# Gated linear attention and a GELU MLP in one kernel: seven products of zeros instead of five ahead of the first prefix sums

## The chip, the core and the metric

The kernel runs on one core of a Trainium2 chip. The metric is device time in microseconds (us) for one execution, lower is better. The engines that matter here are TensorE (PE in the profile; PEld is its loading of the stationary operand, which overlaps the products), VectorE (DVE), ScalarE (ACT), GpSimd (POOL), and SyncE (SP), which only issues transfers. Each engine works through its own instructions in the order of the program; between engines they wait on semaphores.

## What is computed

```python
def attention(q, k, v, alpha):              # each (4, 8, 768, 48): batch, heads, tokens, head size
    for t in range(S):
        state = alpha[:, :, t, :, None] * state + einsum('bhd,bhe->bhde', k[:, :, t], v[:, :, t])
        y[:, :, t] = einsum('bhd,bhde->bhe', q[:, :, t], state)

x = y.transpose(0, 2, 1, 3).reshape(3072, 384)
out = gelu_tanh(x @ w_in) @ w_out           # w_in 384x2048, w_out 2048x384
```

The inputs and the output are float32.

## The kernel before

The tokens are cut into six chunks of 128. A chunk of two batches is a unit `m` (twelve of them, numbered in order of work; unit 0 is chunk 0 with batches 0 and 1, unit 1 is chunk 0 with batches 2 and 3). The recurrence is turned into products inside a chunk, with a carried state between chunks. For one unit the steps are, with the names that the order below uses:

- `ln`: ACT takes the logarithm of alpha, into `la` (line 349 for the first two units, which are packed differently from the rest, line 351 otherwise).
- `cum`: TensorE multiplies `la` by a triangular matrix of ones, which gives prefix sums over the tokens in `cum` (lines 336 and 340 for the first two units, seven products of up to 384 columns and four of 4 columns for one batch).
- `b`, `binv`, `bend`: ACT takes exponentials of `cum` (lines 397 and 391).
- `qp`, `kp`: DVE scales q by `b` and k by `binv` (line 408).
- `t` and `ev`: TensorE transposes `qp` and `kp` into `qkT_ps` (line 418), and ACT or DVE copies the result to `qkT` (line 436).
- `attn` and `mask`: TensorE forms the products of k and q (line 479), DVE masks them (line 486).
- `y`, `x`, `tx`, `xe`, `kv`, `st`: the output of the chunk, its transpose for the MLP, and the new state.
- `l1`, `gelu`, `l2`: the two layers of the MLP (lines 562, 568, 581), which fill most of the rest of the time.

The number behind a name is the unit, the one after the point is the batch in the unit or a running number, so `cum0.1` is the second prefix sum of unit 0.

`Scheduler.order` decides what each engine does next. For the first part of the kernel it does not decide: it follows a list that is written out by hand, `FIRST`, whose letters name the engine (`P` TensorE, `V` DVE, `A` ACT, `G` GpSimd, `S` SyncE). `LANDED` gives the times at which that list takes the loads to have landed; it does not alter the order of the list.

An entry `P:fill.n` in `FIRST` stands for `n` products of a tile of zeros with itself (`fill`, lines 274 to 280: 128x128 by 128x512 into a bank of PSUM with the name `idle`). Nothing reads their result. They take a bank of the ring `ff`, which has four; the prefix sums of the first units and the products of the MLP take banks of the same ring. `fill.5` at the head of the list is TensorE's first work and waits only for the zeros (a memset on DVE, line 849, with the one at line 853 the last that TensorE waits for). The next TensorE work behind it is `cum0.0`, which waits for `ln0.0` on ACT, which waits for the first load of alpha.

The loads: `S:load.0` to `S:load.11` are issued by SP (line 295), in the order a, a, q, k, q, k of unit 0 and the same of unit 1, each 192 KB. `G:load.12` and on are issued by POOL: v of unit 0 behind `gate.0`, then, behind `gate.1`, the first quarter of `w_in`, v of unit 1, the other quarters of `w_in`, `w_out` and the later units. A gate is a copy of one column on POOL (line 304): `gate.0` waits for the second load of alpha, `gate.1` for `qp0.1`, since it reads that tile.

The head of the list, with the entry that the change touches:

```python
FIRST = """
    A:table.0 S:load.0 S:load.1 S:load.2 S:load.3 S:load.4 A:ln0.0 S:load.5 P:fill.5 P:cum0.0 A:ln0.1 G:gate.0 G:load.12 S:load.6 P:cum0.1 A:b0.0 S:load.7
    A:binv0.0 V:qp0.0 A:bend0.0 A:b0.1 V:kp0.0 S:load.8 P:fill.2 P:t0.0 A:bend0.1 A:binv0.1 V:ev0.0 P:t0.1 S:load.9 A:ev0.1 S:load.10 V:qp0.1 P:fill.3
    P:attn0.0 V:kp0.1 P:t0.2 G:gate.1 S:load.11 G:load.13 V:mask0.1 P:fill.1 P:t0.3 G:load.14 A:ev0.3 V:end0.0 V:ev0.2 A:ln1.0 V:mask0.0 P:fill.4
    P:attn0.1 G:load.15 P:cum1.0 V:mask0.2 A:vb0.0 G:load.16 A:ln1.1 V:vb0.1 P:y0.0 V:mask0.3 A:b1.0 P:cum1.1 ...
```

Of the kernel before, what the change touches and what calls it, by code (L numbers as in the profile page):

```python
# [171 lines left out]
class _Kernel:  # L172
# [9 lines left out]
    RINGS = (('a', 0, 0, 1), ('a', 0, 1, 2), ('q', 0, 0, 1), ('k', 0, 0, 1), ('q', 0, 1, 2), ('k', 0, 1, 2),  # L182
             ('a', 1, 0, 1), ('a', 1, 1, 2), ('q', 1, 0, 1), ('k', 1, 0, 1), ('q', 1, 1, 2), ('k', 1, 1, 2))
    FIRST = """
        A:table.0 S:load.0 S:load.1 S:load.2 S:load.3 S:load.4 A:ln0.0 S:load.5 P:fill.5 P:cum0.0 A:ln0.1 G:gate.0 G:load.12 S:load.6 P:cum0.1 A:b0.0 S:load.7
        A:binv0.0 V:qp0.0 A:bend0.0 A:b0.1 V:kp0.0 S:load.8 P:fill.2 P:t0.0 A:bend0.1 A:binv0.1 V:ev0.0 P:t0.1 S:load.9 A:ev0.1 S:load.10 V:qp0.1 P:fill.3
        P:attn0.0 V:kp0.1 P:t0.2 G:gate.1 S:load.11 G:load.13 V:mask0.1 P:fill.1 P:t0.3 G:load.14 A:ev0.3 V:end0.0 V:ev0.2 A:ln1.0 V:mask0.0 P:fill.4
        P:attn0.1 G:load.15 P:cum1.0 V:mask0.2 A:vb0.0 G:load.16 A:ln1.1 V:vb0.1 P:y0.0 V:mask0.3 A:b1.0 P:cum1.1 G:load.17 A:x0.0 V:qp1.0 A:binv1.0 P:y0.1
# [711 lines left out]
```

## Time and profile before

| | us |
|---|---|
| median of six runs | 179.56 (179.27 to 179.81) |
| the profiled execution, its own time | 179.5 |
| span of the profile, first to last instruction | 177.7 |
| PE busy / PEld busy | 171.8 / 136.0 |
| ACT busy | 131.0 |
| DVE busy | 95.0 |
| POOL busy | 57.8 |

The span is 1.8 us shorter than the execution's own time. The times in the views below are counted from the start of the span. A timeline row gives the start, the time from the start of its first instruction to the end of its last, the engine, the line, the operation, what it writes and reads, the shape and the number of instructions merged in the row; in brackets stands how long the engine had been idle before it and what ended that. The products of TensorE are pipelined, so one that follows another starts before the other's end: the time from one start to the next is shorter than the duration of one. A row of the windows gives, for a stretch of the span, the busy time of PE, PEld, DVE, ACT and POOL with the number of instructions, the granted clock of TensorE, the busy share of the DMA engines and GB/s.

### The profile page before, as it was taken

What the parts mean: (1) busy time and instruction counts of PE and PEld (TensorE: products, weight loads), DVE (VectorE), ACT (ScalarE), POOL (GpSimd) and SP (SyncE); (2) the same over time, 40 slices, a digit from 0 to 9 for tenths busy, and PEclk for the clock granted to TensorE, in tenths of its full rate; (3) what the DMA queues carried; (4) which work ended last, traced back from release to release, by engine and by line L of the source; (5) the groups of instructions that cost most, each with busy time, mean ns of one, the idle gap of its engine ahead of it and who ended that gap; (6) DMA issues with size and microseconds to landing.
All of it is one profiled execution on the core that took longest, in us unless ns stands there. A gap on an engine that the chain in (4) does not pass through costs nothing.

```text
span 177.7 us, 4411 instructions
## 1 busy us (share of the span) xinstructions
PE 171.8 (97%) x1831; PEld 136.0 (77%) x1831; DVE 95.0 (53%) x187; ACT 131.0 (74%) x216; POOL 57.8 (33%) x64
## 2 busy tenths in 40 slices
PE   5999999999999999999999999999999999999992
PEld 1656899666896897798698689688697697786972
DVE  6299820354967894596499797495426405000000
ACT  4567899875898668858788967977988984481831
POOL 2379336987635775767640000000000000000000
PEclk9999999999999999999999999999999999999999
DMA  4999999999999999999999993271270360401102
GB/s 118 263 271 189 194 224 233 238 245 195 237 286 203 222 266 217 196 250 212 194 252 235 196 158 93 57 175 48 46 208 4 89 162 4 130 3 48 44 3 85
DMA packets 48900, 28.86 MB, mean 162 GB/s; under 512 B 37488, under 2 KB 45296, under 8 KB 48880
## 3 DMA queue, kind: packets, MB, share of 16 engines
q0 software_dynamic: 26464, 17.70, 60.7%
q1 hardware_dynamic: 22416, 10.88, 24.9%
q8 instruction: 14, 0.23, 0.6%
q14 instruction: 6, 0.05, 0.1%
HBM read 25.17 MB, written 4.72 MB: 168 GB/s over the span
## 4 chain that ended last, share of the span: by engine, by line
PE 89%; ACT 3%; DVE 3%; DMA 2%; issue 1%; DVEq 0%
PE acc L581 35%; PE hT L562 34%; PE at L479 4%; PE qkT_ps L418 3%; PE yps L536 2%; PE yps L533 2%; PE cum L368 2%; PE kv L496 2%; DMA a<-in_alpha_dram 2%; PE cum L336 2%; DVE atm L486 1%; ACT qkT L436 1%; PE xT_ps L550 1%; PE idle L279 1%; ACT L568 1%
## 5 line engine op out<-in xcount | busy, mean ns | idle before, releaser
L581 PE MATMUL acc<-w_out,gT 128*128 128x384 bf16 (+1 forms) x400 | 69.4, 319 | 0.0
L562 PE MATMUL hT<-xT,w_in 128*128 128x256 bf16 x576 | 68.8, 273 | 0.1
L568 ACT ACTIVATE gT<-hT 128x512 bf16<-128x512 f32 x96 | 56.1, 599 | 15.1 <-PE hT L562 11.6
L562 PEld LDWEIGHTS <-w_in 128*128 128x128 bf16 x576 | 61.2, 114 | 1.5 <-issue 0.2
L581 PEld LDWEIGHTS <-gT 128*128 128x128 bf16 x400 | 36.5, 97 | 18.9
L486 DVE TENSOR_TENSOR atm<-at,ut 128x512 bf16<-128x512 f32 x48 | 30.1, 683 | 13.7 <-PE at L479 13.7
L408 DVE TENSOR_TENSOR qp<-q,b 128x768 bf16<-128x768 f32 (+1 forms) x15 | 11.9, 795 | 17.9 <-ACT b L397 17.9
L593 ACT COPY ot<-acc 128x384 f32<-128x384 f32 (+1 forms) x18 | 8.3, 461 | 13.7 <-PE acc L581 11.5
L298 POOL DMA_DIRECT2D k<-in_k_dram x11 | 12.2, 1105 | 9.1 <-DVE atm L486 3.0
L298 POOL DMA_DIRECT2D a<-in_alpha_dram x11 | 12.2, 1112 | 5.8 <-DMA w_in<-in_moe_w_in_dram 1.4
L298 POOL DMA_DIRECT2D q<-in_q_dram x11 | 12.2, 1108 | 5.3 <-issue 1.0
L298 POOL DMA_DIRECT2D vb<-in_v_dram x11 | 12.1, 1100 | 4.9 <-DMA a<-in_alpha_dram 1.2
L397 ACT ACTIVATE b<-cum 128x768 bf16<-128x768 f32 (+1 forms) x15 | 10.3, 685 | 3.3 <-PE cum L340 1.6
L270 ACT ACT_TABLE_LOAD x9 | 11.5, 1283 | 0.9 <-PEq L884 0.7
L408 DVE TENSOR_TENSOR kp<-k,binv 128x768 bf16<-128x768 f32 (+1 forms) x15 | 11.9, 791 | 0.0
L568 ACT ACT_TABLE_LOAD x9 | 11.5, 1283 | 0.2
L397 ACT ACTIVATE binv<-cum 128x768 bf16<-128x768 f32 (+1 forms) x15 | 10.2, 680 | 0.0
L518 DVE TENSOR_TENSOR stmp<-kv,st 128x384 f32<-128x384 f32 x16 | 8.8, 553 | 2.0 <-PE kv L496 2.0
L543 DVE CAST x<-yps 128x384 bf16<-128x384 f32 x12 | 6.7, 558 | 5.2 <-PE yps L536 5.2
L521 DVE TENSOR_TENSOR st<-stmp,ends 128x384 bf16<-128x384 f32 x16 | 8.9, 558 | 0.6
L436 ACT COPY qkT<-qkT_ps 128x512 bf16<-128x512 bf16 (+1 forms) x9 | 6.5, 729 | 3.4 <-PE qkT_ps L418 3.4
L351 ACT ACTIVATE la<-a 128x768 f16<-128x768 f32 (+1 forms) x11 | 8.5, 784 | 0.6 <-DMA a<-in_alpha_dram 0.5
(64 smaller groups left out, 159.0 us busy)
## 6 DMA issues: line engine op xcount, KB each, us to landing
out_dram<-ot SPq DMA_DIRECT2D x23, 192.0 KB, 2.4
a<-in_alpha_dram POOLq DMA_DIRECT2D x9, 384.0 KB, 11.8
q<-in_q_dram POOLq DMA_DIRECT2D x9, 384.0 KB, 11.7
k<-in_k_dram POOLq DMA_DIRECT2D x9, 384.0 KB, 11.7
vb<-in_v_dram POOLq DMA_DIRECT2D x9, 192.0 KB, 11.8
w_in<-in_moe_w_in_dram POOLq DMA_DIRECT2D x4, 384.0 KB, 8.7
w_out<-in_moe_w_out_dram POOLq DMA_DIRECT2D x4, 384.0 KB, 11.0
a<-in_alpha_dram SPq DMA_DIRECT2D x4, 192.0 KB, 4.1
```

The costliest lines, as they stand in the source:

```text
L270: nc.scalar.add_instruction(mybir.InstLoadActFuncSet(name=nc.get_next_instruction_name(), act_func_set_id=i, engine=mybir.EngineType.Activ ...
L298: dma(u[t][:, lo:hi].rearrange("t b h d -> t (b h) d"), src.rearrange("b h s d -> s (b h) d")[c * C:(c + 1) * C])
L351: self.nc.scalar.activation(u["la"][:, lo:hi, :, 0:self.D], u["a"][:, lo:hi], AF.Ln)
L397: self.nc.scalar.activation(u[n].rearrange("t i h d -> t i (h d)")[:, lo:hi], cum, AF.Exp, scale=1.0 if n == "b" else -1.0)
L408: self.nc.vector.tensor_tensor(out, rows, b, op=ALU.mult)
L486: self.nc.vector.tensor_tensor(u["atm", i][:, o], u["at", i][o], self.ut[:, None, :].to_broadcast([self.C, self.H // 2, self.C]), op=ALU.mult)
L518: nc.vector.tensor_tensor(s, acc, old, op=ALU.add)
L521: nc.vector.tensor_tensor(new.rearrange("f p (o d) -> f (p o) d", o=2), acc.rearrange("f p (o d) -> f (p o) d", o=2), ends, op=ALU.mult)
L562: self.nc.tensor.matmul(h[:, s], w_in[:, j, nt % 4 + s], self.xT[c % self.NX][:, j, lo:hi].rearrange("p g t -> p (g t)"), start=j == 0, st ...
L568: return lambda e: self.nc.scalar.activation(self.gT[c % self.NG][:, nt:nt + 2, lo * self.C:hi * self.C], f.pop(("h", c, lo, nt)), AF.Gelu ...
L581: self.nc.tensor.matmul(f["acc", c, b][:, lo:hi], self.gT[c % self.NG][:, nt, b * self.C:(b + 1) * self.C], self.w_out[:, nt, lo:hi], star ...
L593: self.copy(e)(f["ot", c, b][:, sl], f["acc", c, b] if half is None else f["acc", c, b, half][:, sl])
```

## The change

One number in the list is altered. The two added products come directly behind the five, ahead of `cum0.0`; TensorE gets four more instructions (two loads of the stationary operand and two products). No other engine's instructions are changed, and the order of everything else on TensorE is the same.

```diff
     FIRST = """
-        A:table.0 S:load.0 S:load.1 S:load.2 S:load.3 S:load.4 A:ln0.0 S:load.5 P:fill.5 P:cum0.0 A:ln0.1 G:gate.0 G:load.12 S:load.6 P:cum0.1 A:b0.0 S:load.7
+        A:table.0 S:load.0 S:load.1 S:load.2 S:load.3 S:load.4 A:ln0.0 S:load.5 P:fill.7 P:cum0.0 A:ln0.1 G:gate.0 G:load.12 S:load.6 P:cum0.1 A:b0.0 S:load.7
```

## The prediction

> **What bounds the kernel now.** I read the page's slices first.
>
> ```profile
> PE   5999999999999999999999999999999999999992
> PEclk9999999999999999999999999999999999999999
> ```
>
> TensorE has work in nearly every slice, so whatever delays it early is likely to reach the end. The clock row says full speed everywhere, but it can't be taken at its word for the first slices: the durations of equal work, in the timeline of TensorE alone, contradict it.
>
> ```profile
> 1.19 2.31 PE L279 MATMUL idle<-zero 128*128 128x512 bf16 x5 [1.19 <-DVE half L853]
> 4.39 1.44 PE L336 MATMUL cum<-la,ut_blk 128*128 128x384 f16 x7 [0.89 <-ACT la L349]
> 5.62 0.29 PE L340 MATMUL cum<-blk,la 128*128 128x4 f16 x4
> 5.77 1.44 PE L336 MATMUL cum<-la,ut_blk 128*128 128x384 f16 x7
> 7.00 0.29 PE L340 MATMUL cum<-blk,la 128*128 128x4 f16 x4
> 7.16 1.01 PE L279 MATMUL idle<-zero 128*128 128x512 bf16 x2
> 7.96 0.63 PE L418 MATMUL qkT_ps<-ident,qp 128*128 128x128 bf16 x4
> 8.39 0.52 PE L418 MATMUL qkT_ps<-ident,kp 128*128 128x128 bf16 x4
> 8.74 0.81 PE L279 MATMUL idle<-zero 128*128 128x512 bf16 x3
> ...
> 10.36 0.39 PE L418 MATMUL qkT_ps<-ident,kp 128*128 128x128 bf16 x4
> ...
> 11.93 0.83 PE L336 MATMUL cum<-la,ut_blk 128*128 128x384 f16 x7
> 12.60 0.24 PE L340 MATMUL cum<-blk,la 128*128 128x4 f16 x4
> 12.70 0.36 PE L536 MATMUL yps<-vb,atm 128*128 128x48 bf16 x8
> ```
>
> Seven products of one prefix sum take 1.44 us at 4.39 and 5.77 and 0.83 us at 11.93; four transposes take 0.63 at 7.96 and 0.39 at 10.36. Product by product, zeros start 0.427 us apart ahead of 3 us and 0.216 apart behind 8.74; in the row at 8.39 the last two transposes start 0.086 apart, between 0.107 before and 0.056 after. So TensorE runs at half speed until about 8.65 us, inside that row, and at full speed from there.
>
> Whether the early part counts at all, the chain that ended last and the windows tell.
>
> ```profile
> 0.74 3.06 DMA a<-in_alpha_dram
> 3.81 0.53 ACT la L349
> 4.39 1.44 PE cum L336 x7
> 5.91 1.30 PE cum L336 x7
> 7.29 0.88 PE idle L279 x2
> 8.17 0.44 PE qkT_ps L418 x4
> ```
>
> ```profile
> 23.19:120.00 96.81, 96.81 (x1099) 78.41 (x1099) 64.32 (x117) 78.05 (x125) 45.49 (x41) 1.00 1.21 208
> 120.00:174.00 54.00, 54.00 (x513) 43.52 (x511) 13.22 (x21) 37.22 (x59) 0.00 (x0) 1.00 0.25 68
> ```
>
> The chain starts with alpha's first load, then runs over both half-speed prefix sums and zeros into the transposes. From 23.19 TensorE has no idle time up to 174 us. A shift that survives to 23.19 comes through to the end.
>
> **The two products by themselves.** Five take 0.427 us from start to start ((2.31 - 0.63) / 4, 0.63 being one product's duration). The fifth starts at 2.87 and hands over at 3.30; two more end their turn at 3.30 + 2 x 0.427 = 4.15. `cum0.0` starts at 4.39, released by `ln0.0`. So 0.24 us of idle time is left, and the 0.85 us of added work is hidden under the wait for alpha (landed 3.79) and its logarithm (3.81 + 0.52). They wait for no bank (four in the ring, one taken). Direct cost: 0. Without that cover, with alpha over 0.24 us earlier, the excess would be paid, at most 0.85.
>
> **What they may move: the clock.** From 4.39 to 8.65, 4.26 us, TensorE was busy without a break, and then the clock rose. From 1.19 to 4.39 it had the five products, then a break of 1.09 (3.30 to 4.39), and the clock did not rise. With seven the break is 0.24. If a stretch of continuous work is what counts, and a break of 0.24 does not spoil it, the same 4.26 us now run from 1.19 and end at 5.45. The bounds: 5.45, or 8.65 again if the short break spoils it too. I take 5.45: the work from 5.62 to 5.77 and from 7.00 to 7.16 is four products of 4 columns each, in which the array is nearly empty for 0.15 us, and twice that did not prevent the rise at 8.65, so breaks of that size are tolerated.
>
> The Trainium skill (TensorE: Matmul & The Clock Gate, Part 1, What's actually happening) gives a rule beside this: the clock is raised after one busy window of 3413 ns, and the windows run freely, whatever the kernel does. By it the rise at 8.65 makes 5.24 the previous boundary of this execution, with the break of 1.09 in the window ahead of it; with seven that window has 0.24 idle and the rise would come at 5.24, which gives the same sum within 0.1 us. It speaks against a fixed gain, though: in another execution the boundary lies elsewhere, in both kernels, and the same section warns not to fit to a count of cold products. No run here shows that spread yet.
>
> **What an earlier clock is worth,** from 5.45. Of `cum0.0` 0.32 us are left; at full speed about 0.19: 0.13 gained. `cum0.1` with its small products takes 5.77 to 7.16, 1.39; the same work at full speed takes 11.93 to 12.70, 0.77: 0.62 gained, 0.75 in all. TensorE comes to the two zeros at 6.41 and leaves them at 6.84 (2 x 0.216). Here the next limit appears: `qp0.0` on DVE waits for `b0.0`, only 0.13 earlier, and ends at 6.47 - 0.13 + 0.56 = 6.90. So `t0.0` starts at about 6.95 instead of 7.96; `kp0.0` ends at 7.36, so `t0.1` starts at 7.40 and is done at 7.79 (0.39 each). ACT's copy starts at 7.83 instead of 8.95 and `attn0.0` at 8.47 instead of 9.59; DVE's copy starts at 7.40 instead of 8.63, and `qp0.1` at 8.01 instead of 9.24 (q landed 7.20). TensorE is some 1.1 us early at `attn0.0`.
>
> **What takes part of it back: loads.** The loads do not move with TensorE.
>
> ```profile
> 10.41 0.75 POOL L311 DMA_DIRECT2D w_in<-in_moe_w_in_dram  x1
> ...
> 11.70 0.50 ACT L379 CAST vb<-v 128x384 bf16<-128x384 f32 x1
> ...
> 12.10 0.52 ACT L349 ACTIVATE la<-a 128x384 f16<-128x384 f32 x1
> ```
>
> By the trace's landing events the last parts of v of unit 0 land at 11.10 and of the second alpha of unit 1 at 11.49. So `vb0.0` can move from 11.70 to 11.12 and `ln1.1` behind it from 12.10 to 11.52, ending at 12.04. `cum1.1` behind that starts at 12.08 instead of 12.90: 0.82 early, no longer 1.1.
>
> Those landings may slip: POOL's `gate.1` waits for `qp0.1`, so the first quarter of `w_in` is issued 1.23 earlier, 9.18 instead of 10.41, and its packets (which began some 1.2 us behind the issue) meet SP's loads. Bounds for alpha's delay: 0, if `w_in`'s packets stay behind v's, which were put on the same queue and end at 11.10; or 1.6 us, if SP's queue falls from 10.4 on to the 40% of its rate (59 against 165 KB per half us) that it had from 12.0 to 12.5, when `w_in` came up, so that the last 1.1 us take 2.7. The nearer is 0, since half of v's shares end after 10.2; I take 0.25. That leaves 0.82 - 0.25 = 0.57, about 0.6 us. Behind 13 us the chain is compute; the later weights come no later than before. The bounds of this step: 1.1 gained, or 1.0 lost (1.6 less the 0.6 of slack of `ln1.1` behind alpha).
>
> **The sum.** 179.5 - 0.6 = 178.9 us, 0.3% faster. The median of the runs is 0.06 above the profiled execution, which I leave out.
>
> **The rivals.** *Nothing moves:* the products vanish in the idle time and the clock rises where it did: 179.5. For it: the break is not fully closed, and no row shows what a 0.24 us break of no work at all does. Against: the 0.15 us stretches above. The same time comes out if the rise is early but loads eat all of it.
>
> *The loads collide (slower):* the early `gate.1` lets `w_in` run into alpha of unit 1. It decides from the point at which alpha lands later than 12.10, 0.61 behind its present 11.49; from there `ln1.1` is late, and behind it on ACT `b1.0`, `x0.0` and `binv1.0`, for which DVE's `qp1.0` and TensorE's `cum1.1` wait. With a delay of 1.1, midway between that point and the bound of 1.6, it costs 0.5: 180.0. For it: in the windows the DMA engines are 0.96 to 1.00 busy from 4.39 to 12, so there is no spare rate. Against: the queue order above.
>
> *The zeros overrun:* where alpha comes earlier than in the profiled execution, `cum0.0` waits for the seventh product. Even without any earlier clock that is a few tenths at most: 179.7.
>
> **How the numbers follow.** Forecast 0.60, nothing 0.20, collision 0.14, overrun 0.06. The forecast's own range is 178.4 (1.1 gained, no load in the way) to 179.3. The range over all cases, to hold eight in ten, reaches from 178.4 to 179.8. A measurement of this kernel can tell from no change about 0.2%, 0.36 us. Of the forecast about one tenth falls inside that and the rest is faster: 0.54 faster; nothing with that tenth and half of the overruns: 0.29 within; the rest, 0.17, slower.
>
> **What would show it.** Right: in the profile after, the first row of zeros has seven products ending near 4.35, `cum0.0` still starts near 4.39, `cum0.1` takes about 0.8 us instead of 1.44, the four transposes at about 7 us take 0.39, and `w_in` is issued near 9.2. The load step: `ln1.1` starts between 11.5 and 12. Wrong: `cum0.1` again at 1.44 (the clock did not come), `cum0.0` later than 4.45 (overrun), or the ACT row of `ln1.1` behind 12.1 with a wait for alpha (collision). A start of the long stretch of `l1` products no earlier than 23.19, in spite of an early clock, would mean that I have missed a wait between 13 and 23 us.

## The result, and the profile after

| | median, us | runs |
|---|---|---|
| before, five products | 179.44 (178.88 to 180.76) | 48 |
| after, seven products | 178.57 (177.74 to 180.00) | 24 |

The ratio is 0.995, with a 95% interval from 0.9938 to 0.9961: 0.5% faster, about 0.9 us. The profiled execution took 178.72 us, its span is 176.9 us, 0.8 us shorter than the span before.

The timeline of TensorE alone, in the profile after; the columns are start, time from first start to last end, engine, line, operation, tiles, shape, number of instructions:

```profile
1.19 3.17 PE L279 MATMUL idle<-zero 128*128 128x512 bf16 x7 [1.19 <-DVE half L853]
4.29 1.44 PE L336 MATMUL cum<-la,ut_blk 128*128 128x384 f16 x7
5.53 0.29 PE L340 MATMUL cum<-blk,la 128*128 128x4 f16 x4
5.68 1.40 PE L336 MATMUL cum<-la,ut_blk 128*128 128x384 f16 x7
6.91 0.24 PE L340 MATMUL cum<-blk,la 128*128 128x4 f16 x4
7.01 0.59 PE L279 MATMUL idle<-zero 128*128 128x512 bf16 x2
7.44 0.39 PE L418 MATMUL qkT_ps<-ident,qp 128*128 128x128 bf16 x4
7.67 0.39 PE L418 MATMUL qkT_ps<-ident,kp 128*128 128x128 bf16 x4
7.89 0.81 PE L279 MATMUL idle<-zero 128*128 128x512 bf16 x3
8.73 0.40 PE L479 MATMUL at<-qkT 64*128 64x128 bf16 x8
```

Read the durations, as before. The last of the seven products starts at 3.72 and hands over at 4.15, ahead of `cum0.0`, which starts at 4.29, some 0.1 earlier than before because alpha landed 0.09 earlier in this execution (3.70). Both prefix sums still run at half speed (1.44 and 1.40). Everything from 7.01 on runs at full speed: two products of zeros in 0.59 us instead of 1.01, four transposes in 0.39 instead of 0.63. The record of the granted clock in the trace begins at 6.90 us; before it began at 8.65. So the transposes start 0.52 earlier, the next ones 0.72, and `attn0.0` 0.86.

The loads, in the timeline of all engines after:

```profile
9.64 0.75 POOL L311 DMA_DIRECT2D w_in<-in_moe_w_in_dram  x1
...
10.89 0.50 ACT L379 CAST vb<-v 128x384 bf16<-128x384 f32 x1
...
11.29 0.52 ACT L349 ACTIVATE la<-a 128x384 f16<-128x384 f32 x1
```

The weights are issued 0.77 earlier, and neither row on ACT has a bracket, so ACT had not been idle for a load. From 11 us to the end TensorE's work stands 0.77 earlier than before, and that of DVE and ACT with it from 13 us on; TensorE again has no idle time from 23.19 to 173. So the gain is made ahead of 11 us and carried to the end.

One execution of the changed kernel, in its repeat (seven_again below), had a mean granted clock of 0.56 and took 291.74 us; no reading below rests on it.

### The profile page after: what moved, and what is told of

Same layout as the page of the kernel before. It is cut to its first block, busy times and chain, and to the rows that moved or that the text cites. A ratio compares the mean times of both kernels' runs of the same rounds, so it can differ in the third digit from the quotient of the medians.

```text
span 176.9 us, 4415 instructions
## 1 busy us (share of the span) xinstructions
PE 171.9 (97%) x1833; PEld 135.8 (77%) x1833; DVE 95.0 (54%) x187; ACT 130.9 (74%) x216; POOL 57.8 (33%) x64
## 4 chain that ended last, share of the span: by engine, by line
PE 87%; ACT 3%; DVE 3%; DMA 2%; SPq 2%; issue 1%; DVEq 0%
PE acc L581 35%; PE hT L562 35%; PE at L479 4%; PE qkT_ps L418 3%; PE yps L536 2%; DMA k<-in_k_dram 2%; PE yps L533 2%; PE cum L368 2%; PE kv L496 2%; SPq L295 2%; DVE atm L486 1%; ACT qkT L436 1%; PE xT_ps L550 1%; ACT L568 1%; PE cum L370 1%
## 5 line engine op out<-in xcount | busy, mean ns | idle before, releaser
L536 PE MATMUL yps<-vb,atm 128*128 128x48 bf16 x192 | 8.9, 183 | 0.1
L543 ACT CAST x<-yps 128x384 bf16<-128x384 f32 x12 | 5.7, 478 | 4.2 <-PE yps L536 4.2
```

The source lines that it names most:

```text
L536: nc.tensor.matmul(y[:, h, :], u["atm", i][:, h % 2, h // 2, :], u["vb"][:, i, h, :], start=c == 0, stop=True, skip_group_check=True)
L543: self.copy(e)(x, u["y", i].rearrange("t h d -> t (h d)"))
```

## The experiments

Each kernel is the changed one with the edit shown, timed beside the kernel before on the same chip; the ratios are to that kernel.

**One product instead of five.** Is it the amount of work that raises the clock, or its continuity?

```diff
-P:fill.7 P:cum0.0
+P:fill.1 P:cum0.0
```

> One product of zeros ahead of the first prefix sums instead of five, so TensorE rests from about 1.6 to 4.39 us. Theory (the clock rises after a stretch of some 3.4 us in which TensorE is hardly ever idle, and the break of 1.09 us in the kernel before spoils that stretch already): the five products did nothing, so the time stays within 0.25 us of the kernel before, about 179.4 us, and equal work behind 4.39 us has the durations of before. Rival (the clock rises after a certain amount of TensorE work, break or no break): 1.7 us of work less, the rise comes up to 1.7 us later, and the time is 0.4 to 1 us above the kernel before.

Measured: 179.34 us beside 179.41, ratio 0.9995 (0.9981 to 1.0009). Four products fewer than five make no difference, as the theory had it. TensorE alone:

```profile
1.19 0.61 PE L279 MATMUL idle<-zero 128*128 128x512 bf16 x1 [1.19 <-DVE half L853]
4.36 1.44 PE L336 MATMUL cum<-la,ut_blk 128*128 128x384 f16 x7 [2.56 <-ACT la L349]
...
8.37 0.63 PE L418 MATMUL qkT_ps<-ident,kp 128*128 128x128 bf16 x4
```

All of this is at half speed; in this execution the clock rose at 10.35. The rival, the amount of work, had asked for 0.4 to 1 us more than the kernel before, and falls. The five products of the kernel before were worth nothing that can be measured.

**Six, and nine.**

```diff
-P:fill.7 P:cum0.0
+P:fill.6 P:cum0.0      (in the other kernel P:fill.9)
```

> Six products, which leave a break of about 0.66 us ahead of the first prefix sum, where five leave 1.09 and seven 0.24. Theory (a nearly unbroken stretch is what counts): the time lies at that of five (179.4 us) or at that of seven (178.6 us) or between, as the break is or is not tolerated; between the two would mean that it depends on where the stretch falls in an execution. Rival (amount of work): half of the gain of seven, about 179.0 us, with a rise of the clock 0.43 us earlier than with five.

> Nine products: the last ends its turn at 1.19 + 9 x 0.427 = 5.03 us, so the first prefix sum starts 0.64 us later than in the kernel before, unless the clock has risen by then. Theory (unbroken stretch): the clock comes no earlier than with seven, the 0.64 us are paid in part, and the time is between that of seven and that of the kernel before, about 179.0 us. Rival (amount of work): the added work brings the clock forward again and the time is that of seven, 178.6 us, or lower.

Measured: six, 178.51 us, ratio 0.9951 (0.9934 to 0.9969); nine, 178.56 us, ratio 0.9952 (0.9937 to 0.9967). Both have the whole gain. For nine that is the time I had put down for the rival, the amount of work, not for the theory (179.0); in the profile below the rise came so early that the products cost little. Six, TensorE alone:

```profile
1.19 2.74 PE L279 MATMUL idle<-zero 128*128 128x512 bf16 x6 [1.19 <-DVE half L853]
4.31 1.44 PE L336 MATMUL cum<-la,ut_blk 128*128 128x384 f16 x7 [0.38 <-ACT la L349]
...
5.69 0.84 PE L336 MATMUL cum<-la,ut_blk 128*128 128x384 f16 x7
...
7.01 0.40 PE L418 MATMUL qkT_ps<-ident,qp 128*128 128x128 bf16 x4
7.47 0.40 PE L418 MATMUL qkT_ps<-ident,kp 128*128 128x128 bf16 x4
```

Here the second prefix sum already runs at full speed (0.84); the rise is at 5.77. A break of 0.59 us (3.72 to 4.31, from the sixth product's hand-over) is tolerated. The span of this execution is 176.5, 0.4 below that with seven. Nine, TensorE, then ACT, then DVE:

```profile
1.19 3.56 PE L279 MATMUL idle<-zero 128*128 128x512 bf16 x9 [1.19 <-DVE half L853]
4.58 0.82 PE L336 MATMUL cum<-la,ut_blk 128*128 128x384 f16 x7
...
18.96 0.37 PE L536 MATMUL yps<-vb,atm 128*128 128x48 bf16 x8 [0.53 <-DVE vb L379]
```

```profile
10.89 0.51 ACT L379 CAST vb<-v 128x384 bf16<-128x384 f32 x1 [0.38 <-DMA v<-in_v_dram]
```

```profile
18.54 0.36 DVE L379 CAST vb<-v 128x384 bf16<-128x384 f32 x1 [0.67 <-DMA v<-in_v_dram]
```

The rise is at 4.14, ahead of both prefix sums, which take 0.82 each. Nine should have been 0.64 us late; the early rise shortened the last products, and `cum0.0` starts 0.29 later than with seven. Now ACT waits 0.38 us for v of unit 0. That wait is made good: at 17 us TensorE is 1.38 ahead of the kernel before, as at `attn0.0`. What is lost is lost later: v of unit 1 lands at 18.52 (17.45 with seven), DVE waits 0.67 for it and TensorE 0.53 for DVE. From 23 us on 0.97 is left, and the span is 176.8, only 0.2 below that with seven. Loads do limit the gain, as I had predicted for seven, but at an earlier rise and through a later load.

**Four products, started later.** Less work than before, and a short break.

```diff
-nc.vector.memset(self.zero, 0.0)                          (first on DVE)
 nc.vector.tensor_reduce(self.blk, ...)
+nc.vector.memset(self.zero, 0.0)                          (behind the reduction)
-P:fill.7 P:cum0.0
+P:fill.4 P:cum0.0
```

> Four products instead of five, but they start later: the tile of zeros is cleared behind the reduction for blk on DVE instead of first, so that they run from about 2.4 to 4.1 us and the break ahead of the first prefix sum is about 0.25 us instead of 1.09. Less work than the kernel before, without the break. Theory (unbroken stretch): the clock rises earlier than before in most executions, though later than with seven, since the stretch begins 1.2 us later; the time is about half way, 178.8 to 179.1 us. Rival (amount of work): one product less than before, 179.4 us or above.

Measured: 178.87 us, ratio 0.9969 (0.9953 to 0.9985), inside the range of the theory. TensorE alone:

```profile
2.47 1.89 PE L279 MATMUL idle<-zero 128*128 128x512 bf16 x4 [2.47 <-DVE zero L856]
4.34 1.44 PE L336 MATMUL cum<-la,ut_blk 128*128 128x384 f16 x7
...
7.10 0.59 PE L279 MATMUL idle<-zero 128*128 128x512 bf16 x2
7.53 0.38 PE L418 MATMUL qkT_ps<-ident,qp 128*128 128x128 bf16 x4
```

Four products with a break of 0.2 us (the last hands over at 4.15) do more than five with one of 1.09. Together with the single product this shows that the length of the break counts and not the amount of work.

**Weights released too early.** How dear is the collision that I named as the slower rival?

```diff
-'gateqp 0 1'
+'gateqp 0 0'
```

> Seven products, and the gate in front of the weights on POOL reads the first q product of unit 0 instead of the second, so that the first quarter of w_in is issued near 7.2 us instead of 9.6. It measures the collision that I named as the slower rival. If weights that come early do delay alpha of unit 1 (the rival), alpha lands later than 11.5 and ACT waits for it: 0.3 to 1 us slower than seven. If the queue order protects it (my forecast's choice, 0.25 us of delay): within 0.3 us of seven.

Measured: twelve runs from 178.92 to 184.57 us, median 181.73, beside 179.50 for the kernel before on that chip; the five fastest of the twelve alone give a ratio of 1.0038 (1.0007 to 1.0069). The weights were issued at 7.36. The profiled execution (183.99 us), ACT, DVE and then TensorE:

```profile
11.38 0.51 ACT L379 CAST vb<-v 128x384 bf16<-128x384 f32 x1 [0.79 <-DMA v<-in_v_dram]
```

```profile
16.07 0.56 DVE L408 TENSOR_TENSOR qp<-q,b 128x384 bf16<-128x384 f32 x1 [0.89 <-DMA q<-in_q_dram]
19.09 0.56 DVE L408 TENSOR_TENSOR kp<-k,binv 128x384 bf16<-128x384 f32 x1 [2.46 <-DMA k<-in_k_dram]
```

```profile
16.01 0.40 PE L479 MATMUL at<-qkT 64*128 64x128 bf16 x8 [0.19 <-ACT qkT L436]
19.70 0.61 PE L418 MATMUL qkT_ps<-ident,kp 128*128 128x128 bf16 x4 [3.29 <-DVE kp L408]
```

Alpha is late too (it landed at 11.79, against 10.94 after), and ACT waits 0.79 us for v of unit 0. But the dear part is what stands behind alpha on SP's queue: the last k of unit 1 landed at 18.99 instead of 12.98. TensorE waits 3.29 us for it, and its next four transposes take 0.61, half speed again. The windows of that execution, cut at the clock's grid (PE busy, PEld, DVE, ACT, POOL, granted clock, DMA share, GB/s):

```profile
15.44:18.85 3.41, 0.79 (x13) 0.28 (x9) 0.56 (x1) 1.01 (x2) 1.63 (x2) 1.00 1.19 205
18.85:22.27 3.42, 2.57 (x20) 2.20 (x21) 1.84 (x4) 1.07 (x2) 1.03 (x2) 0.50 1.21 210
22.27:25.68 3.41, 3.41 (x37) 2.65 (x36) 2.11 (x4) 2.36 (x5) 1.46 (x2) 0.50 1.08 243
```

After a stretch in which TensorE was busy for 0.79 of 3.41 us the clock is at 0.50 for two stretches, 6.83 us; the first of the two was 75% busy (2.57 of 3.42) and did not bring full speed back, the second, wholly busy, did. In eight of the twelve runs the mean granted clock was 0.98 to 0.99, in the other four 1.00, and these four are the fastest (178.92 to 180.74 us). The collision is real and larger than I priced it. Weights issued at 9.64 (seven) and 8.87 (nine) do not reach it, with the last k at 12.98 and 12.80; weights issued at 7.36 do.

**The zeros in front of the transposes left out.**

```diff
-P:cum0.1 ... P:fill.2 P:t0.0
+P:cum0.1 ... P:t0.0
```

> Seven products at the head, and the two products of zeros between the second prefix sum and the first transposes are left out. Where the clock rises behind about 6.5 us those two stood in the way of the transposes (in the first profile of the changed kernel the transposes started at 7.44, and q's product had been ready at 6.93); where it rises earlier there is slack. Theory: 0.1 to 0.3 us below seven in the median. Rival (they keep the array busy, and without them the clock rises later or falls again): no gain or slower than seven, with four transposes at 0.63 us.

> The changed kernel once more, as the reference for the three others on this chip. 178.5 us, 0.4 to 0.6% below the kernel before; the clock rises at another time than the 6.90 us of its first profile, anywhere from 4.4 to 7.8 us.

Measured: 178.72 us, ratio 0.9952 (0.9936 to 0.9968), beside 178.70, ratio 0.9942 (0.992 to 0.9964), for the changed kernel on that chip, whose rise was not measured a second time. No gain: the rival's time, though not by its mechanism, since the transposes take 0.38 and 0.40. The profile says where the gain went: its rise is at 6.92, almost that of the profile after, and the transposes start at 7.02 instead of 7.44. From 13 to 18 us it is 0.42 ahead. Then TensorE meets v of unit 1 (landed 18.32, against 17.45) and the second quarter of `w_in` (20.25, against 19.20); from 23 us on it is 0.23 ahead, from 35 us 0.05, and at 102 us it falls 0.65 behind. The waits of TensorE from 24 to 176 us (who waited for whom, us in total, times, longest):

```profile
PE hT L562 <- DMA xT<-x: 0.5, 1, 0.5
```

So a gain can be given back to transfers, here to loads and to a transpose by DMA (`turn_x_dma`, line 462) that is used from unit 6 on. That is one execution; the runs show only that the median did not fall.

**Small products.** What does the clock count, time or columns?

```diff
+for _ in range(8 if n == 5 else 0):
+    self.nc.tensor.matmul(ps[:, 0:4], self.zero[:, 0:self.C], self.zero[:, 0:4], start=True, stop=True)
-P:fill.7 P:cum0.0
+P:fill.5 P:cum0.0
```

> Five products of 512 columns and behind them eight of 4 columns with the same weights, so that TensorE has instructions until about 4.1 us, but hardly a column streams through the array in the last 0.85 us. Theory A (the gate counts time in which TensorE has work of any kind, weight loads included): as with seven, 178.5 us. Theory B (it counts streaming columns): as with five, 179.4 us.

Measured: 180.69 us, ratio 1.0056 (1.0033 to 1.008): slower than five, which neither theory had. It does not answer the question. TensorE alone:

```profile
3.30 0.40 PE L281 MATMUL idle<-zero 128*128 128x4 bf16 x8
4.30 1.44 PE L338 MATMUL cum<-la,ut_blk 128*128 128x384 f16 x7 [0.61 <-DVE ut L866]
```

The eight took 0.40 us instead of 0.85, so a break of 0.6 was left (it ends where DVE's `ut` and ACT's logarithm do, both near 4.25); the rise in the profile, 7.36, can't tell the two theories apart, since the stretch of 3.41 us ahead of it begins behind the small products. And the time is not lost there: the early part is 0.2 us behind that of seven, and then TensorE waits at 102 us for the transfer that the last experiment met:

```profile
PE hT L564 <- DMA xT<-x: 1.1, 1, 1.1
```

Why that transfer is later in this kernel is open.

**Without transposes by DMA.** Does the gain depend on those transfers, and does the earlier gate cost anything? All transposes go to TensorE, once with five, once with seven products, and with seven and a later gate.

```diff
-TURN_QK, TURN_X = (7, 8, 9, 10, 11), (6, 7, 8, 9, 10, 11)
+TURN_QK, TURN_X = (), ()
-P:fill.7 P:cum0.0
+P:fill.5 P:cum0.0      (pe5 only)
-'gateqp 0 1'
+'gatekp 0 1'           (pe7_late_gate only)
```

> The kernel before with all its transposes on TensorE (TURN_QK and TURN_X empty), five products of zeros: the partner of the next kernel. The part ahead of about 60 us is the same work in the same order. TensorE gets more work later, some 5 to 8 us, so about 186 us. It is a second profile of the early part with five products: if the clock rises on a grid of about 3.4 us that runs freely, at another time than 8.65, anywhere from 7.2 to 10.7 us.

> The same with seven products. Theory (the gain is made ahead of 13 us and TensorE's later work carries it to the end, whatever that work is): 0.7 to 1.0 us faster than its partner with five, and the clock rises between 4.1 and 7.4 us. Rival (later waits for transfers take the gain or make it): a difference below 0.3 us, or above 1.5.

> Seven products, all transposes on TensorE, and the gate in front of the weights on POOL waits for the second k product of unit 0 instead of the second q product, which is 0.47 us later on DVE, so the weights meet less of SP's loads. If the earlier opening of the gate costs the seven something (the 0.25 us of the prediction's load step), this is 0.1 to 0.3 us faster than its partner with seven; if not, the same within 0.2 us or a little slower.

| | median, us | runs | ratio to the kernel before |
|---|---|---|---|
| pe5 | 185.54 (185.33 to 185.73) | 4 | 1.0336 (1.0321 to 1.035) |
| pe7 | 184.78 (184.55 to 185.44) | 5 | 1.0305 (1.0286 to 1.0324) |
| pe7_late_gate | 185.07 (184.96 to 185.31) | 4 | 1.0311 (1.0297 to 1.0326) |

By the medians seven are 0.76 us faster than five in this kernel too; with so few runs the intervals of the two just overlap. In the two profiles seven are 0.64 ahead at 24 us and 0.76 from 40 us on. So the gain does not need the transposes by DMA. Holding the weights back (10.07 instead of 9.20 in the profiles) gains nothing that can be seen, though 0.1 us would not be seen with so few runs. Five products, and then seven:

```profile
5.72 1.44 PE L336 MATMUL cum<-la,ut_blk 128*128 128x384 f16 x7
...
7.64 0.39 PE L418 MATMUL qkT_ps<-ident,qp 128*128 128x128 bf16 x4
```

```profile
5.68 0.82 PE L336 MATMUL cum<-la,ut_blk 128*128 128x384 f16 x7
...
6.99 0.40 PE L418 MATMUL qkT_ps<-ident,qp 128*128 128x128 bf16 x4
```

With five the clock rose at 7.34 this time, not at 8.65, and with seven at 5.60, not at 6.90.

**All profiles together.** The record of the clock in the trace gives each rise; the stretches at full and at half clock that follow last whole multiples of 3.4133 us (167.253, 170.666, 174.080 and 177.493 us are 49 to 52 times that; 6.827 at half clock in early_gate is twice). So I cut each profile backwards from its rise in steps of 3.41 us, and worked out how much of a stretch TensorE was busy: all of it, less the time before the zeros start (1.19, in late4 2.47) and between the last zeros' hand-over and `cum0.0`. The small products of small8 count as busy here (as idle they would make 62% of the 74%).

| kernel | rise, us | stretch ahead of the rise busy | stretch before that busy |
|---|---|---|---|
| before, five | 8.65 | 100% | 68% |
| pe5, five | 7.34 | 88% | 62% |
| fill1 | 10.35 | 100% | 75% |
| fill6 | 5.77 | 83% | 34% |
| after, seven | 6.90 | 96% | 67% |
| pe7, seven | 5.60 | 95% | 29% |
| pe7_late_gate, seven | 6.80 | 96% | 65% |
| early_gate, seven | 5.20 | 95% | 17% |
| seven_no2 | 6.92 | 96% | 68% |
| fill9 | 4.14 | 86% | none |
| late4 | 7.04 | 94% | 34% |
| small8 | 7.36 | 90% | 74% |

In these profiles the clock rises at the end of a stretch that was busy for 83% or more, and not after one of 75% or less, and where the stretches fall differs from one execution to the next. From the start of unbroken work to the rise it took from 2.95 us (fill9) to 5.99 us (fill1), so a fixed time of work does not fit. That agrees with the rule that the prediction took from the Trainium skill (TensorE: Matmul & The Clock Gate, Part 1, What's actually happening), windows of 3413 ns that run freely; the share between 75% and 83% is this case's. A table of the same section says that the clock falls after an idle window; in early_gate a window that was 23% busy was enough (0.79 of 3.41), so it need not be wholly idle.

Where no later wait takes a larger part back, the span follows the rise: 178.1 us in fill1 (10.35), 177.7 before (8.65), 177.1 in late4 (7.04), 176.9 after (6.90), 176.5 in fill6 (5.77), about 0.35 us for each us, an estimate from these five.

Further profiles of the two kernels as they stand, and the later gate on the changed kernel itself, were planned and gave no result. So each kernel has one profile, and how often the rise falls where is not measured.

## Why the prediction was right

Starts in us, the prediction beside two profiles. Six products had an execution with a rise near the one that I had assumed, so they test the working; seven are the kernel that it was made for.

| step | before | predicted | seven | six |
|---|---|---|---|---|
| rise of the clock | 8.65 | 5.45 | 6.90 | 5.77 |
| `t0.0` | 7.96 | 6.95 | 7.44 | 7.01 |
| `t0.1` | 8.39 | 7.40 | 7.67 | 7.47 |
| `attn0.0` | 9.59 | 8.47 | 8.73 | 8.55 |
| `w_in` issued | 10.41 | 9.18 | 9.64 | 9.21 |
| `ln1.1` on ACT | 12.10 | 11.77 | 11.29 | 11.06 |
| span | 177.7 | 177.1 | 176.9 | 176.5 |

- *The two products by themselves:* right. They hand over at 4.15, as worked out, ahead of `cum0.0`, which starts no later (4.29). (The quotient in the working, (2.31 - 0.63) / 4, is 0.42; the starts in the trace are 0.427 apart, and the sum holds with that.)
- *The clock:* right in kind. A break of 0.14 (seven, 4.15 to 4.29) or 0.59 (six) does not spoil the stretch, one of 1.09 does, and the amount of work does not matter (fill1, late4). My date, 4.26 us of work from 1.19 on, was wrong as a rule: the rise falls on a grid that runs freely, and in the profiles with six products or more, or with the late four, it comes anywhere from 4.1 to 7.0 us. By the sign that I had named, `cum0.1` at 0.8 us, the profile with seven looks like a failure: it took 1.40. The clock came 1.45 us later than 5.45, and still 1.75 us earlier than before. That the rise falls on such a grid stood in the sentences on the skill's page; the sum did without them.
- *What an earlier clock is worth:* right. With the rise at 5.77 each step ahead of the loads is within 0.1 us of the working, and 1.2 us came through to the end of the span. With the rise at 6.90 it was 0.77, of which some 0.1 was there at `cum0.0` already, by alpha's earlier landing.
- *The loads take part of it back:* this step failed. I let v and alpha stay at 11.10 and 11.49 and added 0.25 us for the collision. In the profile after they landed at 10.52 and 10.94, and in fill1, whose weights are issued at 10.38 as before, at 10.61 and 10.83 (pe5: 10.79 and 10.73): the late landings belonged to the one execution that I read, not to the kernel. In the profile with seven the loads took nothing back. A limit exists and binds when the rise is at 4.14 (fill9), but mainly by v of unit 1: of 1.38 us at 17 us 0.97 is left at 23 us. So "behind 13 us the chain is compute" does not hold there, nor in seven_no2.
- *The sum:* 0.6 forecast, 0.77 in the profiles and 0.87 between the medians. The load term was too large by 0.53 (1.1 to 0.57); the date of the clock, earlier than in this execution, was worth 0.33 too much (1.1 to 0.77) and hid part of that. That the two errors point in opposite directions is luck.
- *The rivals:* nothing moving is ruled out by the interval. The overrun costs less than I said, since a rise ahead of 5 us shortens it (fill9). The collision was named with the wrong main victim (the last k of unit 1 more than alpha) and too low a price, since the wait of 3.29 us was followed by 6.83 us at half clock (early_gate). Its upper bound was also worked out with 40%, where 59 of 165 KB is 36%; that makes 2.0 us instead of 1.6.

## What to carry to other kernels

Read TensorE's clock in the first microseconds from the durations of equal work, not from a clock row that begins with the first record. Products of zeros ahead of the first real work paid here only if they shortened the break to it far enough: six, with 0.59 us left, gave the whole gain, five, with 1.09, nothing, and four that started late some 0.5 of 0.9 us. How much arrives at the end depends on the next loads. Take landing times from several executions before you let one of them cap a gain.

## What was not expected of the hardware

A break of 1.0 to 1.1 us ahead of the first prefix sum cost the whole gain and one of 0.59 nothing in the median, a step of one product (fill6 against the kernel before). A wait of 3.29 us in the middle of the kernel brought the clock down to 0.50 for 6.83 us (early_gate), so that late data cost more than their delay.
